# Loading K and V by whole batches in a one-core decode kernel: 2 MB transfers with 16 KB rows, and P written with zeros between its head groups

## The chip, the cores and the metric

The kernel runs on one core of a Trainium2 chip. Its time is the device time of one execution in microseconds (us); three executions of the kernel before gave 121.77, 121.84 and 121.88, a median of 121.84 us. Engine names: PE does matrix products (PEld is its weight load), DVE is the vector engine, ACT the scalar engine, POOL the third elementwise engine, SP the engine that issues most transfers.

## What is computed

One decode step for 8 batches: a layer norm, attention over the last 1024 positions of a cache (32 query heads on 8 key/value heads of 128 elements), a gated feed-forward network, and a product of the two. All inputs are bf16.

```python
W = min(4096, max(256, Sk // 4))                       # Sk = 4096, so W = 1024
q = (x @ wq).reshape(B, Sq, Hq, Dh)                    # x: 8 x 1 x 512, normalised; wq: 512 x 4096
k = jnp.repeat(k_cache[:, :, Sk - W:, :], rep, axis=1) # cache: 8 x 8 x 4096 x 128, rep = 4
v = jnp.repeat(v_cache[:, :, Sk - W:, :], rep, axis=1)
p = _softmax(jnp.einsum("bhqd,bhkd->bhqk", q, k) * (Dh ** -0.5))
s = jnp.einsum("bhqk,bhkd->bhqd", p, v).reshape(B, Sq, Hq * Dh) @ wo
g = _silu((_gelu(xn @ w_gate) * (xn @ w_up)) @ w_down) # F = 1792
out = x + s * g
```

Each batch brings 2 MB of K and 2 MB of V (MB here is 2^20 bytes where transfers are counted), wq and wo are 4 MB each, the three FFN weights 1.75 MB each: 47.5 million bytes in all, each read once.

## The kernel before, in words

**Storage.** A ring of 16 slots of 128 partitions by 8 KB (1 MB) takes everything that comes by a large transfer. The 8 key/value heads are split into two groups g of 4 (HG = 4, NG = 2). A transfer of `load_cache` (L71) brings one group of K or V of one batch: partition p holds 32 consecutive positions of one head, an 8 KB row. wq comes as four transfers of 1 MB (L94), one for each slice k of the contraction; gate, up and down in two transfers of 0.875 MB each (L425, L433), wo in three of 1 MB and three smaller pieces of the last (L443). SP issues them in the order K0, wq, K1, V0, K2, V1, K3, V2, ... K7, V6, V7, gate, up, down, wo. A transfer waits for the last reader of its slot, and also for the landing of the transfer eight before it, because eight completion semaphores go round.

**Order of the work.** The schedule is written out by hand (`manual_schedule`): each engine executes its instructions in the order of the program text, so an instruction that waits holds up everything behind it on its engine.

**Query.** 32 products of 128x512 (L247) build q in eight PSUM banks, slice k after slice k. Copies to bf16 (L256), DVE transposes (L259) and 16 small copies (L268, by DVE and ACT) make `qbd`, the stationary operand of the scores.

**A batch b** takes these steps:

- `turn_k(b, g)` (L235): a DVE transpose in 32x32 blocks turns a 1 MB group of K, read as 2048 words of 32 bits a partition, into `kT`. Three kT buffers.
- `scores(b, g)` (L283, L294): one masking product for each half of the 1024 columns of S with g = 0, then 8 products of 128x512 for each group. S is 128 partitions x 1024 columns in PSUM; a partition is one query head and one of 4 parts of the window.
- `softmax(b)`: the maximum of each row on DVE (L304), two small DVE steps across the four parts (L309, L311), four small ACT instructions that write the negative maximum `nb` (L314), then one ACT exponential of 128x1024 (L316) that writes P and its sums.
- `turn_p(b)` (L327): a DVE transpose of P, 512 words a partition.
- `values(b)` (L338): 64 products of 128x128. `keep_o` (L351) copies the result to SBUF, `gather` (L359, L363) sums the parts on PE, and after four batches `regroup` (L374 to L390) normalises on DVE, makes 8 small products and casts into `oT`.

The loop's order around the change:

```python
    for b in range(B):
        if b + 2 < B:
            load_k(b + 2)
        if b + 1 < B:
            load_v(b + 1)
            turn_k(b + 1, 0)
        softmax(b)
        if b + 1 < B:
            scores(b + 1, 0)
        if b >= 1:
            gather(b - 1)
        if b + 1 < B:
            turn_k(b + 1, 1)
            scores(b + 1, 1)
        turn_p(b); values(b); keep_o(b)
        if b == 4:
            regroup(0)
```

**Tail.** After the last batch PE does gather(7) and regroup(1), then the products z and u of the FFN (L457, 16 each), waits for the gelu chain on ACT and DVE (L467 to L480), does the 56 products of f (L486), and last the 128 products of s (L505), 32 for each megabyte of wo in the order of its pieces. Two DVE steps (L513, L515) and the output transfer (L517) end the kernel.

Of the kernel before, what the change touches and what calls it, by code (L numbers as in the profile page):

```python
# [7 lines left out]
ACT = mybir.ActivationFunctionType  # L8
# [7 lines left out]
N_SLOTS = 16  # L16
# [5 lines left out]
def kernel(  # L22
# [27 lines left out]
    C = W * HG // P  # L50
    ROW = C * Dh
    FT = F // 4
# [16 lines left out]
    def load_cache(cache, b, g, name):  # L69
        t = slot(name)  # L70
        nc.sync.dma_start(  # L71
            out=t,
            in_=cache[b, g * HG : (g + 1) * HG, win0:Sk, :].rearrange(
                "n (p c) d -> p n (c d)", c=C
            ),
        )
        return t
# [3 lines left out]
    def load_k(b):  # L81
        for g in range(NG):
            k_sb[b, g] = load_cache(A_k_cache, b, g, "k_sb")

    def load_v(b):
        for g in range(NG):
            v_sb[b, g] = load_cache(A_v_cache, b, g, "v_sb")
# [4 lines left out]
    for k in range(NK):  # L92
        t = slot("wq_sb")
        nc.sync.dma_start(out=t, in_=wq_v[:, k, :])  # L94
        wq_sb.append(t)
# [109 lines left out]
    sel = consts.tile([P, NG, Hq], FP32, name="sel")  # L205
    nc.vector.memset(sel, 0.0)
    for g in range(NG):
        nc.vector.tensor_reduce(
            out=sel[:, g, g * qd : (g + 1) * qd],
            in_=ident.rearrange("p (t g h) -> p g h t", t=4, g=NG)[:, g],  # L210
            axis=AX.X,
            op=ALU.add,
        )
# [19 lines left out]
    def turn_k(b, g):  # L233
        t = kT_pool.tile([P, ROW], BF16, name="kT")
        nc.vector.transpose(out=t.bitcast(I32), in_=k_sb[b, g].bitcast(I32))  # L235
        kT[b, g] = t
# [4 lines left out]
    q_bf = slot("q_bf")  # L241
    q_t = slot("q_t")
    with tc.tile_pool(name="ps_q", bufs=1, space=PSUM) as ps_q:
        q_ps = [ps_q.tile([P, 512], FP32, name=f"q_ps{i}") for i in range(8)]
        for k in range(NK):
            for i in range(8):
                nc.tensor.matmul(  # L247
                    q_ps[i],
                    xnR[:, k, :, :].rearrange("p j b -> p (j b)"),
                    wq_sb[k][:, i * 512 : (i + 1) * 512],  # L250
                    start=(k == 0),
                    stop=(k == NK - 1),
                )
        for i in range(8):
            e = nc.vector.tensor_copy if i % 2 else nc.scalar.copy
            e(out=q_bf[:, i * 512 : (i + 1) * 512], in_=q_ps[i])  # L256
            if i % 2:
                sl = slice((i - 1) * 512, (i + 1) * 512)
                nc.vector.transpose(out=q_t[:, sl].bitcast(I32), in_=q_bf[:, sl].bitcast(I32))  # L259

    q_v = q_t.rearrange("p (g h m b r w) -> p m b r w g h", g=NG, h=qd, m=2, b=B, r=RB)
    for j in range(4):
        sl = slice(32 * j, 32 * j + 32)
        for m in range(2):
            e = (nc.vector.tensor_copy, nc.scalar.copy)[(j + m) % 2]
            for g in range(NG):
                c0 = j * Hq + g * qd
                e(out=qbd[sl, m, :, :, g, c0 : c0 + qd], in_=q_v[sl, m, :, 0, :, g, :])  # L268
# [3 lines left out]
    sums = keep.tile([P, B], FP32, name="sums")  # L272
# [6 lines left out]
    def scores(b, g):  # L279
        if g == 0:  # L280
            S[b] = ps_s.tile([P, 2, 512], FP32, name="S_ps")
            for half in range(2):
                nc.tensor.matmul(  # L283
                    S[b][:, half, :],
                    neg_st.rearrange("p j h -> p (j h)"),
                    neg_mv.rearrange("p a n -> p (a n)"),
                    start=True,
                    stop=False,
                )
        kv = kT[b, g].rearrange("p (c m i w) -> p c m i w", m=2, i=32, w=2)  # L290
        for m in range(2):
            for w in range(2):
                for half in range(2):
                    nc.tensor.matmul(  # L294
                        S[b][:, half, :],
                        qbd[:, m, b, w, g, :],
                        kv[:, half * 16 : (half + 1) * 16, m, :, w],
                        start=False,
                        stop=(g == NG - 1 and m == 1 and w == 1),
                    )  # L300

    def softmax(b):
        mx = two.tile([P, 1], FP32, name="mx")
        nc.vector.tensor_reduce(  # L304
            out=mx, in_=S[b].rearrange("p a c -> p (a c)"), axis=AX.X, op=ALU.max
        )

        m2 = two.tile([64, 1], FP32, name="m2")
        nc.vector.tensor_tensor(out=m2, in0=mx[0:64, :], in1=mx[64:128, :], op=ALU.max)  # L309
        m1 = two.tile([32, 1], FP32, name="m1")  # L310
        nc.vector.tensor_tensor(out=m1, in0=m2[0:32, :], in1=m2[32:64, :], op=ALU.max)  # L311
        nb = two.tile([P, 1], FP32, name="nb")
        for j in range(4):
            nc.scalar.mul(nb[32 * j : 32 * j + 32, :], m1, -inv)  # L314
        P_sb[b] = two.tile([P, C // 2, 32, 2], BF16, name="P_sb")
        nc.scalar.activation(  # L316
            out=P_sb[b].rearrange("p c i w -> p c w i"),
            in_=S[b].rearrange("p a (c w i) -> p (a c) w i", w=2, i=32),
            func=ACT.Exp,
            bias=nb,  # L320
            scale=inv,
            accum_out=sums[:, b : b + 1],
        )

    def turn_p(b):
        pT[b] = two.tile([P, C // 2, Hq, 2], BF16, name="pT")
        nc.vector.transpose(  # L327
            out=pT[b].rearrange("p c h w -> p (c h w)").bitcast(I32),
            in_=P_sb[b].rearrange("p c i w -> p (c i w)").bitcast(I32),
        )  # L330

    def values(b):
        O_ps[b] = ps_o.tile([P, NG, Dh], FP32, name="O_ps")
        for g in range(NG):
            vv = v_sb[b, g].rearrange("p (c d) -> p c d", d=Dh)
            for c in range(C):
                t = c % 4
                nc.tensor.matmul(  # L338
                    O_ps[b][32 * t : 32 * t + 32, g, :],
                    pT[b][:, c // 2, :, c % 2],  # L340
                    vv[:, c, :],
                    start=(c < 4),
                    stop=(c >= C - 4),
                )
# [4 lines left out]
    def keep_o(b):  # L349
        O_sb[b] = two.tile([P, NG, Dh], FP32, name="O_sb")  # L350
        nc.scalar.copy(out=O_sb[b], in_=O_ps[b])  # L351

    def gather(b):
        q = b % 4
        if q == 0:
            o_ps[b // 4] = ps_g.tile([P, Dh + 1], FP32, name="o_ps")
        o = o_ps[b // 4][32 * q : 32 * q + 32, :]
        for g in range(NG):
            nc.tensor.matmul(  # L359
                o[:, 0:Dh], sel[:, g, :], O_sb[b][:, g, :], start=(g == 0), stop=(g == NG - 1)  # L360
            )
        for g in range(NG):
            nc.tensor.matmul(  # L363
                o[:, Dh : Dh + 1],
                sel[:, g, :],
                sums[:, b : b + 1],
                start=(g == 0),
                stop=(g == NG - 1),
            )

    def regroup(q):

        rc = two.tile([P, 1], FP32, name="rc")
        nc.vector.reciprocal(out=rc, in_=o_ps[q][:, Dh : Dh + 1])  # L374
# [21 lines left out]
    scores(0, 1)  # L396
    for b in range(B):
        if b + 2 < B:
            load_k(b + 2)
        if b + 1 < B:  # L400
            load_v(b + 1)
            turn_k(b + 1, 0)
        softmax(b)
        if b + 1 < B:
            scores(b + 1, 0)
        if b >= 1:
            gather(b - 1)
        if b + 1 < B:
            turn_k(b + 1, 1)
            scores(b + 1, 1)  # L410
# [7 lines left out]
    HR = NK // 2  # L418
    wgu = []
    for w in (B_w_gate, B_w_up):  # L420
        wv = w.rearrange("(p k) f -> p k f", k=NK)
        for i in range(2):
            t = slot("wgu_sb")
            tv = t[:, 0 : HR * F].rearrange("p (k f) -> p k f", k=HR)
            nc.sync.dma_start(out=tv, in_=wv[:, i * HR : (i + 1) * HR, :])  # L425
            wgu.append(tv)
    wd = []
    wdv = B_w_down.rearrange("(p j) d -> p j d", j=NJ)
    for i in range(2):
        t = slot("wd_sb")  # L430
        n = NJ // 2
        tv = t[:, 0 : n * D].rearrange("p (j d) -> p j d", d=D)
        nc.sync.dma_start(out=tv, in_=wdv[:, i * n : (i + 1) * n, :])  # L433
        wd.append(tv)
    wo = []
    for u in range(NU):
        t = slot("wo_sb").rearrange("p (j d) -> p j d", d=D)
# [15 lines left out]
    for n, ws in (("z_ps", wgu[0:2]), ("u_ps", wgu[2:4])):  # L453
        ps = ps_f.tile([P, FT], FP32, name=n)
        for k in range(NK):
            for t in range(4):
# [3 lines left out]
                    ws[k // HR][:, k % HR, t * FT : (t + 1) * FT],  # L460
# [23 lines left out]
    for j in range(NJ):  # L484
        for t in range(4):
# [3 lines left out]
                wd[j // (NJ // 2)][:, j % (NJ // 2), t * DT : (t + 1) * DT],  # L489
# [60 lines left out]
```

## Time and profile before

| what | value |
|---|---|
| device time, median of 3 executions | 121.84 us (121.77 to 121.88) |
| the profiled execution: span from its first to its last instruction | 119.9 us (119.85) |
| median less that span: what lies around the instructions | 1.99 us |
| PE busy, DVE busy, ACT busy | 72.9, 76.5, 32.3 us |
| transfers on SP's queue, share of 16 DMA engines' span | 94.5% |
| bytes moved | 47.46 million, 396 GB/s over the span |
| from issue to landing of a 1 MB K or V transfer, median | 19.6 us |
| slowest engine of 16: landing of K6 whole, of K7 whole, of V7 whole | 73.53, 83.35, 93.15 us |

No device time of the profiled execution itself is listed apart from its span, so the 1.99 us are counted as constant. The landings are the times of the completion semaphores' last updates in the trace, from the span's start. In the page's rows "busy, mean ns" are of a group of equal instructions; "idle before" is the idle time of the engine ahead of them and what ended it. In timeline rows the first column is the start and the second the length, in us; a bracket holds the idle time before.

### The profile page before, as it was taken

Reading aid. Unit: us, or ns where it says so; the run is one execution under the profiler, and the core shown is the slowest. Engines: PE = TensorE matmul, PEld = TensorE weight load, DVE = VectorE, ACT = ScalarE, POOL = GpSimd, SP = SyncE. Lnnn points to the kernel's source line nnn. Section 1 sums busy time; section 2 is a strip of 40 time slices with the busy share of each in tenths; the row PEclk is TensorE's granted clock in tenths of the full one; section 3 lists DMA queues with packets and bytes.
Section 4 is the critical chain, followed back from the end, with each engine's and each line's share of the span. In section 5 each row is a group of like instructions: output and inputs, shape, how many; then the busy total and the mean of one; then the engine's idle time right before and its main releaser. Section 6 shows DMA issues by size and latency. Waiting matters only on the chain.

```text
span 119.9 us, 2323 instructions
## 1 busy us (share of the span) xinstructions
PE 72.9 (61%) x992; PEld 38.0 (32%) x992; DVE 76.5 (64%) x100; ACT 32.3 (27%) x76; POOL 3.2 (3%) x10
## 2 busy tenths in 40 slices
PE   0103999033994997969687684992692547353460
PEld 0101333001341543535443351450352432052440
DVE  3698824999039999999959959909951253720010
ACT  4600005358007052341712510700608101100000
POOL 2250000000000000000000000000000000000000
PEclk9999999955589999999999999599999855555555
DMA  2999999999999999999999999999999999999920
GB/s 90 399 410 427 429 435 418 429 427 435 413 432 429 427 424 418 432 427 421 424 427 427 432 421 416 429 432 429 413 427 432 423 419 419 433 433 418 403 109 3
DMA packets 6974, 47.61 MB, mean 397 GB/s; under 512 B 812, under 2 KB 948, under 8 KB 1972
## 3 DMA queue, kind: packets, MB, share of 16 engines
q1 hardware_dynamic: 6948, 47.46, 94.5%
q8 instruction: 7, 0.11, 0.3%
q14 instruction: 3, 0.02, 0.0%
q10 hardware_dynamic: 16, 0.01, 0.0%
HBM read 47.46 MB, written 0.01 MB: 396 GB/s over the span
## 4 chain that ended last, share of the span: by engine, by line
DMA 52%; DVE 19%; PE 15%; ACT 8%; issue 1%; SPq 1%; DVEq 0%
DMA k_sb<-in_A_k_cache_dram 16%; DMA wgu_sb<-in_B_w_up_dram 16%; DMA wo_sb<-in_A_wo_dram 13%; DVE kT L235 7%; DMA wq_sb<-in_A_wq_dram 7%; PE q_ps L247 7%; PE S_ps L294 7%; DVE mx L304 4%; ACT P_sb L316 4%; ACT qbd L268 3%; DVE q_t L259 2%; DVE q_bf L256 2%; ACT nb L314 2%; DVE pT L327 2%; SPq L71 1%
## 5 line engine op out<-in xcount | busy, mean ns | idle before, releaser
L294 PE MATMUL S_ps<-kT,qbd 128*128 128x512 bf16 x128 | 33.5, 408 | 15.7 <-DVE kT L235 12.3
L235 DVE STREAM_TRANSPOSE kT<-k_sb 128x2048 int32<-128x2048 int32 x16 | 36.5, 2289 | 4.3 <-DMA k_sb<-in_A_k_cache_dram 4.2
L294 PEld LDWEIGHTS <-qbd 128*128 128x128 bf16 x128 | 12.9, 102 | 33.2 <-issue 17.0
L247 PE MATMUL q_ps<-wq_sb,xnR 128*128 128x512 bf16 x32 | 9.9, 483 | 6.2 <-DMA wq_sb<-in_A_wq_dram 6.2
L304 DVE TENSOR_REDUCE mx<-S_ps 128x1 f32<-128x1024 f32 x8 | 9.6, 1195 | 5.9 <-PE S_ps L294 5.9
L314 ACT ACTIVATE nb<-m 32x1 f32<-32x1 f32 x32 | 6.4, 201 | 21.9 <-DVE m L311 21.7
L316 ACT ACTIVATE P_sb<-S_ps,nb 128x1024 bf16<-128x1024 f32 x8 | 11.1, 1390 | 0.3
L338 PE MATMUL O_ps<-v_sb,pT 128*32 128x128 bf16 x512 | 8.6, 220 | 2.6 <-DVE pT L327 2.6
L351 ACT COPY O_sb<-O_ps 128x256 f32<-128x256 f32 x8 | 3.0, 372 | 22.6 <-PE O_ps L338 22.6
L338 PEld LDWEIGHTS <-pT 128*32 128x32 bf16 x512 | 7.2, 97 | 5.6 <-issue 3.0
L327 DVE STREAM_TRANSPOSE pT<-P_sb 128x512 int32<-128x512 int32 x8 | 5.7, 711 | 3.4 <-ACT P_sb L316 3.3
L283 PE MATMUL S_ps<-neg_mv,neg_st 128*128 128x512 bf16 x16 | 5.2, 410 | 3.8 <-DVE q_bf L256 3.8
L247 PEld LDWEIGHTS <-xnR 128*128 128x128 bf16 x32 | 3.7, 118 | 12.0 <-issue 10.2
L505 PE MATMUL s_ps<-wo_sb,oT 128*32 128x128 bf16 x128 | 4.4, 307 | 4.7 <-DMA wo_sb<-in_A_wo_dram 4.7
L359 PE MATMUL o_ps<-O_sb,sel 128*32 128x128 f32 x32 | 5.9, 314 | 1.0 <-ACT O_sb L351 1.0
L256 ACT CAST q_bf<-q_ps 128x512 bf16<-128x512 f32 x4 | 2.1, 600 | 14.2 <-PE q_ps L247 14.2
L268 ACT COPY qbd<-q_t 32x256 bf16<-32x256 bf16 x8 | 4.7, 622 | 3.3 <-DVE q_t L259 3.3
L513 DVE TENSOR_TENSOR y<-s_ps,g_sb 128x128 f32<-128x128 f32 x1 | 0.3, 292 | 8.1 <-PE s_ps L505 8.1
L505 PEld LDWEIGHTS <-oT 128*32 128x32 bf16 x128 | 3.5, 136 | 5.6 <-issue 5.6
L256 DVE CAST q_bf<-q_ps 128x512 bf16<-128x512 f32 x4 | 2.6, 662 | 3.9 <-PE q_ps L247 3.9
L359 PEld LDWEIGHTS o_ps<-O_sb,sel 128*32 128x32 f32 x32 | 3.2, 121 | 4.4 <-issue 2.1
L240 DVE MEMSET qbd<- 128x4096 uint32 x1 | 3.5, 3472 | 0.8 <-issue 0.8
(64 smaller groups left out, 47.1 us busy)
## 6 DMA issues: line engine op xcount, KB each, us to landing
k_sb<-in_A_k_cache_dram SPq DMA_DIRECT2D x16, 1024.0 KB, 19.6
v_sb<-in_A_v_cache_dram SPq DMA_DIRECT2D x16, 1024.0 KB, 19.6
wq_sb<-in_A_wq_dram SPq DMA_DIRECT2D x4, 1024.0 KB, 11.5
wo_sb<-in_A_wo_dram SPq DMA_DIRECT2D x3, 1024.0 KB, 17.8
wgu_sb<-in_B_w_gate_dram SPq DMA_DIRECT2D x2, 896.0 KB, 19.1
wgu_sb<-in_B_w_up_dram SPq DMA_DIRECT2D x2, 896.0 KB, 18.7
wd_sb<-in_B_w_down_dram SPq DMA_DIRECT2D x2, 896.0 KB, 17.8
wo_sb<-in_A_wo_dram SPq DMA_DIRECT2D x1, 512.0 KB, 16.7
```

The lines of the kernel that those rows point to most:

```text
L235: nc.vector.transpose(out=t.bitcast(I32), in_=k_sb[b, g].bitcast(I32))
L247: nc.tensor.matmul(q_ps[i], xnR[:, k, :, :].rearrange("p j b -> p (j b)"), wq_sb[k][:, i * 512 : (i + 1) * 512], start=(k == 0), stop=(k = ...
L256: e(out=q_bf[:, i * 512 : (i + 1) * 512], in_=q_ps[i])
L268: e(out=qbd[sl, m, :, :, g, c0 : c0 + qd], in_=q_v[sl, m, :, 0, :, g, :])
L294: nc.tensor.matmul(S[b][:, half, :], qbd[:, m, b, w, g, :], kv[:, half * 16 : (half + 1) * 16, m, :, w], start=False, stop=(g == NG - 1 an ...
L304: nc.vector.tensor_reduce(out=mx, in_=S[b].rearrange("p a c -> p (a c)"), axis=AX.X, op=ALU.max)
L314: nc.scalar.mul(nb[32 * j : 32 * j + 32, :], m1, -inv)
L316: nc.scalar.activation(out=P_sb[b].rearrange("p c i w -> p c w i"), in_=S[b].rearrange("p a (c w i) -> p (a c) w i", w=2, i=32), func=ACT.Exp,
L327: nc.vector.transpose(out=pT[b].rearrange("p c h w -> p (c h w)").bitcast(I32), in_=P_sb[b].rearrange("p c i w -> p (c i w)").bitcast(I32),)
L338: nc.tensor.matmul(O_ps[b][32 * t : 32 * t + 32, g, :], pT[b][:, c // 2, :, c % 2], vv[:, c, :], start=(c < 4), stop=(c >= C - 4),)
L359: nc.tensor.matmul(o[:, 0:Dh], sel[:, g, :], O_sb[b][:, g, :], start=(g == 0), stop=(g == NG - 1))
L505: nc.tensor.matmul(s_ps[32 * t : 32 * t + 32, :], oT[:, j, u, :], wo[u][:, j, t * DT : (t + 1) * DT], start=(u == 0 and j == 0), stop=(u = ...
```

## The change

K and V of a batch come in one transfer of 2 MB each: partition p holds 64 positions of one head (a 16 KB row), and the head index runs over 8 values within 128 partitions. The ring has 8 slots of 2 MB. `turn_k(b, half)` takes half of each row, so both halves need the whole transfer. A half now holds keys of both head groups; `scores(b, half)` fills one half of S's columns with 8 products, 4 for each group, whose moving operand runs over 4 neighbouring heads, then steps on. A row of S holds, as before, the scores of one query head with the 4 heads of its own group; in P's layout all 8 heads stand side by side. So the exponential is done twice, once for each group, over all 1024 columns: `nb` has two columns, and the column of the other group is so low that zeros are written (`off`, `mg`). P is twice as long (1024 words a partition in `turn_p`). `values` still makes 64 products, into one 128x128 result; `gather` needs half as many products; `regroup` adds the two sums first.

In the loop, `softmax` is split into `top` and `softmax`; `turn_k(1, 0)` stands ahead of the loop, and in batch b the DVE order is `top(b)`, `turn_k(b+1, 1)`, `turn_k(b+2, 0)`, `turn_p(b)`. wq comes in two transfers of 2 MB, gate, up and down in one of 1.75 MB each, wo in the same six pieces; q's two buffers share a slot, and q's copies and the qbd copies are dealt out differently between ACT and DVE (6 and 2, then 5 and 11).

The diff, cut to its core:

```diff
-N_SLOTS = 16
+N_SLOTS = 8
...
-    C = W * HG // P
+    C = W * Hkv // P
     ROW = C * Dh
+    HALF = ROW // 2
+    KB = 32 // Hkv
...
+            in_=cache[b, :, win0:Sk, :].rearrange("n (p c) d -> p n (c d)", c=C),
...
+    for i in range(2):
+        t = slot("wq_sb").rearrange("p (k n) -> p k n", k=NK // 2)
+        nc.sync.dma_start(out=t, in_=wq_v[:, i * (NK // 2) : (i + 1) * (NK // 2), :])
+        wq_sb += [t[:, k, :] for k in range(NK // 2)]
...
-    def turn_k(b, g):
-        t = kT_pool.tile([P, ROW], BF16, name="kT")
-        nc.vector.transpose(out=t.bitcast(I32), in_=k_sb[b, g].bitcast(I32))
+    def turn_k(b, half):
+        t = kT_pool.tile([P, HALF], BF16, name="kT")
+        nc.vector.transpose(
+            out=t.bitcast(I32), in_=k_sb[b][:, half * HALF : (half + 1) * HALF].bitcast(I32)
+        )
...
-                        kv[:, half * 16 : (half + 1) * 16, m, :, w],
+                        kv[:, :, m, :, g * HG : (g + 1) * HG, w],
...
+        mg = two.tile([Hq, NG], FP32, name="mg")
+        nc.vector.tensor_scalar(
+            out=mg, in0=off, scalar1=m1[:, 0:1], scalar2=-inv, op0=ALU.add, op1=ALU.mult
+        )
+        nb[b] = two.tile([P, NG], FP32, name="nb")
         for j in range(4):
-            nc.scalar.mul(nb[32 * j : 32 * j + 32, :], m1, -inv)
...
+            nc.scalar.copy(out=nb[b][32 * j : 32 * j + 32, :], in_=mg)
+
+    def softmax(b):
+        P_sb[b] = two.tile([P, C // 2, KB, Hkv, 2], BF16, name="P_sb")
+        for g in range(NG):
+            nc.scalar.activation(
+                out=P_sb[b].rearrange("p c k n w -> p w (c k) n")[:, :, :, g * HG : (g + 1) * HG],
+                in_=S[b].rearrange("p w (c n) -> p w c n", n=HG),
+                func=ACT.Exp,
+                bias=nb[b][:, g : g + 1],
+                scale=inv,
+                accum_out=sums[:, b, g : g + 1],
+            )
...
     def regroup(q):
 
         rc = two.tile([P, 1], FP32, name="rc")
-        nc.vector.reciprocal(out=rc, in_=o_ps[q][:, Dh : Dh + 1])
+        nc.vector.tensor_reduce(
+            out=rc, in_=o_ps[q][:, Dh : Dh + NG], axis=AX.X, op=ALU.add
+        )
+        nc.vector.reciprocal(out=rc, in_=rc)
...
     scores(0, 0)
     scores(0, 1)
+    turn_k(1, 0)
     for b in range(B):
         if b + 2 < B:
             load_k(b + 2)
         if b + 1 < B:
             load_v(b + 1)
-            turn_k(b + 1, 0)
+        top(b)
         softmax(b)
         if b + 1 < B:
             scores(b + 1, 0)
+            turn_k(b + 1, 1)
+            scores(b + 1, 1)
+        if b + 2 < B:
+            turn_k(b + 2, 0)
         if b >= 1:
             gather(b - 1)
-        if b + 1 < B:
-            turn_k(b + 1, 1)
-            scores(b + 1, 1)
         turn_p(b)
...
-        for i in range(2):
-            t = slot("wgu_sb")
-            tv = t[:, 0 : HR * F].rearrange("p (k f) -> p k f", k=HR)
-            nc.sync.dma_start(out=tv, in_=wv[:, i * HR : (i + 1) * HR, :])
-            wgu.append(tv)
...
+        tv = slot("wgu_sb")[:, 0 : NK * F].rearrange("p (k f) -> p k f", k=NK)
+        nc.sync.dma_start(out=tv, in_=w.rearrange("(p k) f -> p k f", k=NK))
+        wgu.append(tv)
+    wd = slot("wd_sb")[:, 0 : NJ * D].rearrange("p (j d) -> p j d", d=D)
+    nc.sync.dma_start(out=wd, in_=B_w_down.rearrange("(p j) d -> p j d", j=NJ))
```

More of the change, by code (lines that the diff above doesn't have):

```diff
@@ L67, with load_cache @@
     nc.scalar.dma_start(out=x_sb, in_=A_x.flatten_outer_dims())
-    def load_cache(cache, b, g, name):
+    def load_cache(cache, b, name):
         t = slot(name)
@@ L72, in load_cache @@
             out=t,
-            in_=cache[b, g * HG : (g + 1) * HG, win0:Sk, :].rearrange(
-                "n (p c) d -> p n (c d)", c=C
-            ),
+            in_=cache[b, :, win0:Sk, :].rearrange("n (p c) d -> p n (c d)", c=C),
         )
@@ L81, in load_k @@
     def load_k(b):
-        for g in range(NG):
-            k_sb[b, g] = load_cache(A_k_cache, b, g, "k_sb")
+        k_sb[b] = load_cache(A_k_cache, b, "k_sb")
     def load_v(b):
-        for g in range(NG):
-            v_sb[b, g] = load_cache(A_v_cache, b, g, "v_sb")
+        v_sb[b] = load_cache(A_v_cache, b, "v_sb")
     load_k(0)
@@ L91 @@
     wq_sb = []
[L92 to L95, printed above, removed]
+    for i in range(2):
+        t = slot("wq_sb").rearrange("p (k n) -> p k n", k=NK // 2)
+        nc.sync.dma_start(out=t, in_=wq_v[:, i * (NK // 2) : (i + 1) * (NK // 2), :])
+        wq_sb += [t[:, k, :] for k in range(NK // 2)]
     load_k(1)
@@ L204 @@
     NU = Hq // 8
-    sel = consts.tile([P, NG, Hq], FP32, name="sel")
-    nc.vector.memset(sel, 0.0)
-    for g in range(NG):
[L208 to L212, printed above, removed]
+    sel = consts.tile([P, Hq], FP32, name="sel")
+    nc.vector.tensor_reduce(
+        out=sel, in_=ident.rearrange("p (t h) -> p h t", t=4), axis=AX.X, op=ALU.add
+    )
+    off = consts.tile([Hq, NG], FP32, name="off")
+    nc.vector.memset(off, -NEG)
+    for g in range(NG):
+        nc.gpsimd.affine_select(
+            out=off[:, g : g + 1],
+            in_=off[:, g : g + 1],
+            compare_op=ALU.is_ge,
+            fill=0.0,
+            base=(-qd if g == 0 else qd - 1),
+            pattern=[[0, 1]],
+            channel_multiplier=(1 if g == 0 else -1),
         )
@@ L231 @@
     kT = {}
-    def turn_k(b, g):
-        t = kT_pool.tile([P, ROW], BF16, name="kT")
-        nc.vector.transpose(out=t.bitcast(I32), in_=k_sb[b, g].bitcast(I32))
-        kT[b, g] = t
+    def turn_k(b, half):
[3 more added lines that the diff above has]
+        )
+        kT[b, half] = t
     turn_k(0, 0)
@@ L240 @@
     nc.vector.memset(qbd, 0.0)
-    q_bf = slot("q_bf")
-    q_t = slot("q_t")
+    q_both = slot("q_both")
+    q_bf = q_both[:, 0:HALF]
+    q_t = q_both[:, HALF:ROW]
     with tc.tile_pool(name="ps_q", bufs=1, space=PSUM) as ps_q:
@@ L253 @@
                 )
[L254 to L258, printed above, removed]
+        for half in range(2):
+            for i in range(4 * half, 4 * half + 4):
+                e = nc.vector.tensor_copy if i % 4 == 3 else nc.scalar.copy
+                e(out=q_bf[:, i * 512 : (i + 1) * 512], in_=q_ps[i])
+            for i in range(4 * half, 4 * half + 4, 2):
+                sl = slice(i * 512, (i + 2) * 512)
                 nc.vector.transpose(out=q_t[:, sl].bitcast(I32), in_=q_bf[:, sl].bitcast(I32))
@@ L264 @@
         for m in range(2):
-            e = (nc.vector.tensor_copy, nc.scalar.copy)[(j + m) % 2]
             for g in range(NG):
+                e = nc.scalar.copy if (4 * j + 2 * m + g) % 3 == 2 else nc.vector.tensor_copy
                 c0 = j * Hq + g * qd
@@ L271 @@
     pT, S, P_sb, O_ps = {}, {}, {}, {}
-    sums = keep.tile([P, B], FP32, name="sums")
+    sums = keep.tile([P, B, NG], FP32, name="sums")
     actx = ExitStack()
@@ L277, with scores @@
     ps_g = actx.enter_context(tc.tile_pool(name="ps_g", bufs=1, space=PSUM))
-    def scores(b, g):
-        if g == 0:
+    def scores(b, half):
+        if half == 0:
             S[b] = ps_s.tile([P, 2, 512], FP32, name="S_ps")
[L282 to L293, printed above, removed]
+        nc.tensor.matmul(
+            S[b][:, half, :],
+            neg_st.rearrange("p j h -> p (j h)"),
+            neg_mv.rearrange("p a n -> p (a n)"),
+            start=True,
+            stop=False,
+        )
+        kv = kT[b, half].rearrange("p (c m k n w) -> p c m k n w", m=2, k=KB, n=Hkv, w=2)
+        for g in range(NG):
+            for m in range(2):
+                for w in range(2):
                     nc.tensor.matmul(
@@ L300, in scores, with top @@
                     )
-    def softmax(b):
+    nb = {}
+    def top(b):
         mx = two.tile([P, 1], FP32, name="mx")
@@ L309, in softmax @@
         nc.vector.tensor_tensor(out=m2, in0=mx[0:64, :], in1=mx[64:128, :], op=ALU.max)
-        m1 = two.tile([32, 1], FP32, name="m1")
+        m1 = two.tile([Hq, 1], FP32, name="m1")
         nc.vector.tensor_tensor(out=m1, in0=m2[0:32, :], in1=m2[32:64, :], op=ALU.max)
-        nb = two.tile([P, 1], FP32, name="nb")
-        for j in range(4):
-            nc.scalar.mul(nb[32 * j : 32 * j + 32, :], m1, -inv)
[L315 to L323, printed above, removed]
+        mg = two.tile([Hq, NG], FP32, name="mg")
[3 more added lines that the diff above has]
+        nb[b] = two.tile([P, NG], FP32, name="nb")
+        for j in range(4):
+            nc.scalar.copy(out=nb[b][32 * j : 32 * j + 32, :], in_=mg)
+    def softmax(b):
+        P_sb[b] = two.tile([P, C // 2, KB, Hkv, 2], BF16, name="P_sb")
+        for g in range(NG):
+            nc.scalar.activation(
[5 more added lines that the diff above has]
+                accum_out=sums[:, b, g : g + 1],
+            )
     def turn_p(b):
@@ L328, in turn_p @@
             out=pT[b].rearrange("p c h w -> p (c h w)").bitcast(I32),
-            in_=P_sb[b].rearrange("p c i w -> p (c i w)").bitcast(I32),
+            in_=P_sb[b].rearrange("p c k n w -> p (c k n w)").bitcast(I32),
         )
     def values(b):
[L333 to L344, printed above, removed]
+        O_ps[b] = ps_o.tile([P, Dh], FP32, name="O_ps")
+        vv = v_sb[b].rearrange("p (c d) -> p c d", d=Dh)
+        for c in range(C):
+            t = c % 4
+            nc.tensor.matmul(
+                O_ps[b][32 * t : 32 * t + 32, :],
+                pT[b][:, c % (C // 2), :, c // (C // 2)],
+                vv[:, c, :],
+                start=(c < 4),
+                stop=(c >= C - 4),
+            )
     o_ps = {}
@@ L349, in keep_o @@
     def keep_o(b):
-        O_sb[b] = two.tile([P, NG, Dh], FP32, name="O_sb")
+        O_sb[b] = two.tile([P, Dh], FP32, name="O_sb")
         nc.scalar.copy(out=O_sb[b], in_=O_ps[b])
@@ L355, in gather @@
         if q == 0:
-            o_ps[b // 4] = ps_g.tile([P, Dh + 1], FP32, name="o_ps")
+            o_ps[b // 4] = ps_g.tile([P, Dh + NG], FP32, name="o_ps")
         o = o_ps[b // 4][32 * q : 32 * q + 32, :]
[L358 to L369, printed above, removed]
+        nc.tensor.matmul(o[:, 0:Dh], sel, O_sb[b], start=True, stop=True)
+        nc.tensor.matmul(o[:, Dh : Dh + NG], sel, sums[:, b, :], start=True, stop=True)
     def regroup(q):
         rc = two.tile([P, 1], FP32, name="rc")
-        nc.vector.reciprocal(out=rc, in_=o_ps[q][:, Dh : Dh + 1])
+        nc.vector.tensor_reduce(
+            out=rc, in_=o_ps[q][:, Dh : Dh + NG], axis=AX.X, op=ALU.add
+        )
+        nc.vector.reciprocal(out=rc, in_=rc)
         o_x = two.tile([P, 8, Dh], BF16, name="o_x")
@@ L415 @@
             regroup(0)
-    HR = NK // 2
     wgu = []
     for w in (B_w_gate, B_w_up):
-        wv = w.rearrange("(p k) f -> p k f", k=NK)
-        for i in range(2):
-            t = slot("wgu_sb")
-            tv = t[:, 0 : HR * F].rearrange("p (k f) -> p k f", k=HR)
-            nc.sync.dma_start(out=tv, in_=wv[:, i * HR : (i + 1) * HR, :])
-            wgu.append(tv)
[L427 to L434, printed above, removed]
+        tv = slot("wgu_sb")[:, 0 : NK * F].rearrange("p (k f) -> p k f", k=NK)
[3 more added lines that the diff above has]
+    nc.sync.dma_start(out=wd, in_=B_w_down.rearrange("(p j) d -> p j d", j=NJ))
     wo = []
     for u in range(NU):
-        t = slot("wo_sb").rearrange("p (j d) -> p j d", d=D)
+        if u % 2 == 0:
+            pair = slot("wo_sb").rearrange("p (v j d) -> p v j d", v=2, d=D)
+        t = pair[:, u % 2]
         src = A_wo[u * 1024 : (u + 1) * 1024, :].rearrange("(p j) d -> p j d", j=8)
@@ L452 @@
     zu = []
-    for n, ws in (("z_ps", wgu[0:2]), ("u_ps", wgu[2:4])):
+    for n, ws in (("z_ps", wgu[0]), ("u_ps", wgu[1])):
         ps = ps_f.tile([P, FT], FP32, name=n)
@@ L459 @@
                     xnR[:, k, t, :],
-                    ws[k // HR][:, k % HR, t * FT : (t + 1) * FT],
+                    ws[:, k, t * FT : (t + 1) * FT],
                     start=(k == 0),
@@ L488 @@
                 hT[:, j, :],
-                wd[j // (NJ // 2)][:, j % (NJ // 2), t * DT : (t + 1) * DT],
+                wd[:, j, t * DT : (t + 1) * DT],
                 start=(j == 0),
```

## The prediction, made before the changed kernel was run

> **What bounds the kernel now.** I read the slices of the page first, then the chain in order of time, then DVE's and PE's timeline from 60 us on.
>
> ```profile
> PEclk9999999955589999999999999599999855555555
> DMA  2999999999999999999999999999999999999920
> GB/s 90 399 410 427 429 435 418 429 427 435 413 432 429 427 424 418 432 427 421 424 427 427 432 421 416 429 432 429 413 427 432 423 419 419 433 433 418 403 109 3
> ```
>
> The 16 DMA engines are full from 2 us to 115 us at about 427 GB/s. The time is the start, 47.46 million bytes at that rate, and an end.
>
> ```profile
> 61.38 19.52 DMA k_sb<-in_A_k_cache_dram
> ...
> 80.96 18.73 DMA wgu_sb<-in_B_w_up_dram
> ...
> 99.70 15.93 DMA wo_sb<-in_A_wo_dram
> 115.63 0.04 issue
> 115.67 0.66 PE s_ps L505 x16
> ```
>
> From 61 us the chain is transfers alone, up to the last piece of wo, whose products close it. But compute isn't far behind:
>
> ```profile
> 80.92 2.31 DVE L235 STREAM_TRANSPOSE kT<-k_sb 128x2048 int32<-128x2048 int32 x1 [2.85 <-DMA k_sb<-in_A_k_cache_dram]
> 88.92 1.23 DVE L304 TENSOR_REDUCE mx<-S_ps 128x1 f32<-128x1024 f32 x1 [1.12 <-PE S_ps L294]
> 98.60 1.68 PE L457 MATMUL z_ps<-wgu_sb,xnR 128*32 128x448 bf16 x16
> 105.58 1.68 PE L486 MATMUL f_ps<-wd_sb,hT 128*32 128x128 bf16 x56 [2.68 <-DVE hT L480]
> 108.58 1.04 PE L505 MATMUL s_ps<-wo_sb,oT 128*32 128x128 bf16 x32 [1.31 <-DMA wo_sb<-in_A_wo_dram]
> ```
>
> K7's first megabyte starts the last stretch of attention at 80.92; its FFN begins at 98.60 and ends at 107.26; PE waits only 1.31 us for wo. Without any wait the four parts of s (4 x 1.04 = 4.16) would end at 107.26 + 0.05 + 4.16 = 111.5, against 116.33 in fact. So **the cover of the compute tail is 4.8 us**, and whatever delays z by more sets the end.
>
> **The change, part by part.**
>
> *Transfers.* The trace's packet records show 46, 159 and 309 ns for 1, 4 and 8 KB: 37.6 ns a KB and some 8.4 ns fixed. Landings in the steady stretch are 2.445 us apart for a megabyte (K4 to K6: 19.52 us for 8), where 64 KB an engine at 37.6 ns make 2.405; 0.040 us are fixed. Rows of 16 KB and half the transfers halve that: 36 MB of K, V and wq save 36 x 0.020 = 0.72, the FFN weights 3 x 0.037 = 0.11, together **0.83 us**. Bounds: 0 if a 16 KB row goes as two packets; 1.60 if the packet records' fixed part is saved whole (144 + 24 packets fewer an engine at 8.4 ns, 21 completion packets at 9 ns). I take 0.83, from the landings, which are what others wait for. [...]
>
> *SP's queue.* The count in flight falls from 8 of 1 MB to at most 7 or 8 of 2 MB, and each now waits for its slot's reader alone. The tightest of these: wo's first piece waits for `turn_k(6,1)`, about 84 us below, and its turn on the engines comes about 102. So the rings never run dry; if that cover failed, each missing microsecond would show whole.
>
> *Landing of K.* Before, `turn_k(b,0)` began with the first megabyte (K7: 80.89); now with the second (83.35, less 0.64 = 82.7). That is 1.8 us later for K7, about the same for K6 (71.09; 73.53 - 0.56 = 73.0).
>
> *Start.* wq's first landing moves from 10.86 to 13.37. 16 products at 427 ns would end about 19, wq's rest lands about 18, 16 more at 213 ns end near 21.5 (20.85 before). Copies: six of 0.60 on ACT beside two casts and four transposes on DVE (2 x 0.66 + 4 x 0.71), then qbd 11 x 0.33 on DVE beside 5 x 0.57 on ACT: ends near 29, as before. One masking product moves between the halves, 0.4. All this disappears: DVE waits for K5 and K6 below by 0.7 and 2.3 us.
>
> *A batch on DVE.* `mx` 1.20, m2 and m1 0.155 and 0.147, `mg` new: two columns, 0.16 by those rows; with gaps **top = 1.79**. Two kT of 2.24 (back to back; 2.3 after a wait). pT: from 711 ns for 512 words and 2289 for 2048, 1.03 ns a word, **1.24** for 1024 (bounds 0.71 and 1.42). A batch takes 7.5 instead of the 6.76 between the maxima at 41.87, 48.63 and 55.39.
>
> *ACT.* nb 0.84 stays (4 x 0.20), the exponential of 1.45 runs twice: 0.86 + 2.90 = **3.76**. Bounds of one: 1.39 is the same operation on as many elements; a copy with scattered reads and writes (qbd, 622 ns for 256 columns) takes 1.67 times the contiguous one (O_sb, 372 ns), so up to 2.3; 0.7 if zeros cost nothing. I take 1.45: its output steps by 4 bytes in both kernels. Mid-loop it lies beside two kT (4.48); in batches 6 and 7, with one and none, it is bare.
>
> *PE.* As many S and value products; runs of 4 heads in the moving operand have no row; bounds 1 and 1.37 times (weight load of scattered o_x 162 ns, of xnR 118), hidden in the slack of a batch, since 16 x 0.213 + 0.6 + 1.1 + 0.4 = 5.5 of 7.5. `gather` halves: -0.4, as O_sb's copy -0.1.
>
> *The new wait.* `turn_k(b+2,0)` waits for K(b+2), and `turn_p(b)`, hence values(b), regroup(0) and top(b+1), stand behind it on DVE. DVE comes to `turn_k(6,0)` at 63.2 (K5) + 2.24 + 1.24 + 1.79 + 2.24 = 70.7 and waits until 73.0. From there:
>
> - kT(6,0) 75.3; pT(4) 76.5; regroup(0): two small steps 0.33, o_x 1.28, products 0.71, cast 0.48, and part of values(4) ahead of them at the lower clock: 79.7
> - top(5) 81.5; kT(6,1) 83.7; kT(7,0) 86.0 (K7 landed at 82.7); pT(5) 87.2; top(6) 89.0
> - nb and two exponentials 92.75 (kT(7,1) beside them); pT(6) 94.0; top(7) 95.8; nb and exponentials 99.55; pT(7) 100.8
> - values(7) 1.08 at full clock, double at half; 1.6 taken: 102.4; O_sb, gather, sums, o_x, r_ps: 0.28 + 0.75 + 0.33 + 1.34 + 0.6: z at **105.7**, 7.1 later than 98.60.
>
> From K7's landing alone the same durations give 82.7 + 22.1 = 104.8. Then z to f's end as before, 8.66: 114.4; s 4.2: 118.5, with all of wo landed (115.96 - 0.83). The output's 3.52 us after s stay: span 122.1, against 119.85: **+2.25**. With the 1.99 around it as in the median shown, 121.84 + 2.25 = **124.1 us**.
>
> PE's clock is a second cost. The page shows 5 for PEclk in the slice at 75 us, after 2.2 us of idle PE (71.35 to 73.56), and from 96 us on. Now each K wait leaves it idle about as long or longer. [...] In my sum only values(4), values(7) and gather carry it; s may regain full clock at its end, up to -1.
>
> **Rivals.**
>
> - *Transfers stay last*: 121.84 - 0.83 = 121.0 (120.2 with 1.60). For it: full slices, 4.8 us of cover. It decides when z slips by less than 4.8 - 0.8 = 4.0, z before 102.6. Against it: K7's landing, two bare exponentials and a longer pT allow 104.8; it needs engines' skew at K7 gone (its first engine finished 1.5 us before the last) and cheaper exponentials.
> - *PE or ACT becomes the bound* (slower side): exponentials at 2.3 instead of 1.45 add 1.7 to each of batches 6 and 7, 3.4: 127.5; half clock in scores adds 1.9 for a half batch on the path: 126.
> - *Rows are cut to 8 KB, no gain in transfers*: K6 and K7 land 0.6 later, 124.7; slower just the same.
>
> **How the numbers follow.** Forecast, compute tail last, 122.3 to 125.5: 0.62. PE or ACT bound, 125.5 to 130: 0.20. Transfers last or compute just beside them, 120.2 to 121.6: 0.13. Between, about equal: 0.05. A measurement of this kernel can tell 0.2%, 0.24 us. Faster 0.13, same 0.05, slower 0.82. The range leaves out about half of the first rival and a good third of the second: 121.3 to 127.0.
>
> **What would show it.** Right: PE waits for wo in no part of s; DMA slices fall to 0 while PE still works; DVE waits for K5 and K6 with pT queued behind; two exponentials of 1.4 and pT of 1.24; z at 104 to 107. Packets of 16 KB at 610 ns and K6 landing at 73.0 confirm the first term. Wrong: s still waiting for wo's last piece, or z before 102.6; an exponential or S product far from its row of before.

## The result, and the profile after

The changed kernel took 196.36 us (median of four executions, 195.49 to 198.38) against 121.86 us: a ratio of 1.613, interval 1.603 to 1.623. The forecast was 124.1, with a range up to 127.0. The profiled execution has a span of 194.1 us and took 195.86.

The slices of the page of the changed kernel, each now 4.85 us long:

```profile
PEclk9999997599559755885579559755885699555555
DMA  6999999999999999999999999999999999999980
GB/s 164 216 321 432 327 216 216 216 226 221 223 223 233 216 223 216 216 218 216 216 216 219 216 216 216 216 223 216 216 219 219 216 233 213 359 426 420 430 354 7
```

The DMA engines are as busy as before, at half the rate: 216 to 233 GB/s in nearly every slice. Two stretches stand out: around the fourth slice, where wq comes, and from the 35th on, where the FFN weights and wo come. There it is up to 432. DVE waits for each K from K2 on, for 8.1 to 12.4 us; three of these waits:

```profile
51.36 2.31 DVE L240 STREAM_TRANSPOSE kT<-k_sb 128x2048 int32<-128x2048 int32 x1 [8.14 <-DMA k_sb<-in_A_k_cache_dram]
90.45 2.31 DVE L240 STREAM_TRANSPOSE kT<-k_sb 128x2048 int32<-128x2048 int32 x1 [11.90 <-DMA k_sb<-in_A_k_cache_dram]
109.76 2.31 DVE L240 STREAM_TRANSPOSE kT<-k_sb 128x2048 int32<-128x2048 int32 x1 [11.93 <-DMA k_sb<-in_A_k_cache_dram]
```

The idle time in the bracket, some 12 us for each of K3 to K6, stands where the kernel before waited 1.38 us for K5 and 2.85 for K7 (the row at 80.92 in the prediction):

```profile
61.34 2.31 DVE L235 STREAM_TRANSPOSE kT<-k_sb 128x2048 int32<-128x2048 int32 x1 [1.38 <-DMA k_sb<-in_A_k_cache_dram]
```

The tail of the changed kernel on PE, with the first products of s at its end:

```profile
180.56 1.68 PE L489 MATMUL f_ps<-wd_sb,hT 128*32 128x128 bf16 x56 [2.56 <-DMA wd_sb<-in_B_w_down_dram]
182.98 1.04 PE L508 MATMUL s_ps<-wo_sb,oT 128*32 128x128 bf16 x32 [0.74 <-DMA wo_sb<-in_A_wo_dram]
```

PE waits for the down weights and for wo, so the transfers are last, as before.

**Where the 74.5 us came from.** In the packet records the 16 KB rows of K and V take 1240 ns (median of the steady stretch) where those of wq take 611, and 14 KB rows of the FFN weights 535. K4 landed at 90.43 and K6 at 128.96: 38.53 us for 8 MB, 4.82 a megabyte against 2.445 before. For the 32 MB of K and V that is 32 x 2.37 = 75.9 us more, a little over the whole loss. V7 lands at 167.31 instead of 93.15; from there to the end it is 26.8 us, against 26.7 before.

### The profile page after: what moved, and what is told of

Read it like the earlier page. It is cut to its first block, busy times and chain, and to the rows that moved or that the text cites. A ratio compares the mean times of both kernels' runs of the same rounds, so it can differ in the third digit from the quotient of the medians.

```text
span 194.1 us, 2240 instructions
## 1 busy us (share of the span) xinstructions
PE 78.9 (41%) x953; PEld 41.7 (22%) x960; DVE 81.5 (42%) x110; ACT 39.7 (20%) x91; POOL 3.4 (2%) x12
## 3 DMA queue, kind: packets, MB, share of 16 engines
q1 hardware_dynamic: 3924, 47.46, 96.6%
## 4 chain that ended last, share of the span: by engine, by line
DMA 36%; another core or an unknown queue 36%; DVE 21%; PE 3%; SPq 2%; issue 1%
DMA k_sb<-in_A_k_cache_dram 24%; DVE kT L240 13%; DMA wo_sb<-in_A_wo_dram 12%; DVE pT L344 3%; DVE mx L314 3%; PE O_ps L354 2%; SPq L73 1%; DVE mg L323 1%; SPq L92 1%; DVE m L319 0%; DVE m L321 0%; SPq L446 0%; PE s_ps L508 0%; PE r_ps L396 0%
## 5 line engine op out<-in xcount | busy, mean ns | idle before, releaser
L354 PE MATMUL O_ps<-v_sb,pT 128*32 128x128 bf16 x512 | 14.4, 300 | 74.5 <-DVE pT L344 55.3
L302 PE MATMUL S_ps<-kT,qbd 128*128 128x512 bf16 x128 | 38.6, 453 | 7.4 <-DVE qbd L277 3.6
L354 PEld LDWEIGHTS <-pT 128*32 128x32 bf16 x512 | 12.3, 138 | 75.5 <-DVE pT L344 56.2
L333 ACT ACTIVATE P_sb<-S_ps,nb 128x1024 bf16<-128x1024 f32 x16 | 21.1, 1349 | 0.3
L344 DVE STREAM_TRANSPOSE pT<-P_sb 128x1024 int32<-128x1024 int32 x8 | 9.7, 1214 | 5.3 <-ACT P_sb L333 5.3
L328 ACT COPY nb<-mg 32x2 f32<-32x2 f32 x32 | 6.1, 190 | 12.3 <-DVE mg L323 12.0
L265 ACT CAST q_both<-q_ps 128x512 bf16<-128x512 f32 x6 | 3.0, 611 | 19.8 <-PE q_ps L255 19.8
L374 PE MATMUL o_ps<-O_sb,sel 128*32 128x128 f32 x16 | 3.5, 302 | 0.7 <-ACT O_sb L367 0.7
L277 DVE COPY qbd<-q_both 32x256 bf16<-32x256 bf16 x11 | 3.4, 359 | 0.0
L277 ACT COPY qbd<-q_both 32x256 bf16<-32x256 bf16 x5 | 3.0, 617 | 0.9 <-DVE q_both L268 0.9
```

Of the source, the lines that this page charges most:

```text
L302: nc.tensor.matmul(S[b][:, half, :], qbd[:, m, b, w, g, :], kv[:, :, m, :, g * HG : (g + 1) * HG, w], start=False, stop=(g == NG - 1 and m ...
L328: nc.scalar.copy(out=nb[b][32 * j : 32 * j + 32, :], in_=mg)
L333: nc.scalar.activation(out=P_sb[b].rearrange("p c k n w -> p w (c k) n")[:, :, :, g * HG : (g + 1) * HG], in_=S[b].rearrange("p w (c n) -> ...
L344: nc.vector.transpose(out=pT[b].rearrange("p c h w -> p (c h w)").bitcast(I32), in_=P_sb[b].rearrange("p c k n w -> p (c k n w)").bitcast( ...
L354: nc.tensor.matmul(O_ps[b][32 * t : 32 * t + 32, :], pT[b][:, c % (C // 2), :, c // (C // 2)], vv[:, c, :], start=(c < 4), stop=(c >= C - 4),)
```

## The experiments

The row of 16 KB can't be slow by itself, since wq has it too, at 611 ns. What K and V alone have is the way their rows are laid over the partitions. Three theories: **A**, the grouping of the destination: 16 groups of 8 partitions instead of 32 groups of 4. **B**, long rows of the cache. **C**, the source addresses (16 KB and 1 MB apart) collide.

### Groups of 4 with 16 KB rows

The changed kernel reads 4 heads of 2048 positions instead of 8 heads of 1024; nothing else differs.

```diff
-            in_=cache[b, :, win0:Sk, :].rearrange("n (p c) d -> p n (c d)", c=C),
+            in_=cache[b, 0:4, Sk - 2 * W : Sk, :].rearrange("n (p c) d -> p n (c d)", c=C),
```

> The changed kernel, but each K or V transfer reads 4 heads x 2048 positions instead of 8 heads x 1024: still 2 MB in 16 KB rows, but the destination's 128 partitions are 32 groups of 4 instead of 16 groups of 8. (It reads other cache rows than the reference; the instructions are otherwise the same.) Theory A (the grouping of partitions 16 x 8 halves the rate, because two DMA engines at a time write where only one can): K packets fall from 1240 to about 611 ns, 2 MB land every 4.85 us, and the time is set by the compute tail as predicted, 124.1 us (122.3 to 125.5). Theory B (16 KB rows of the cache are slow themselves, by their length): stays near 196 us, packets 1240 ns. Theory C (the source addresses, 16 KB and 1 MB apart, collide in HBM): the steps are the same here with 4 heads, so it stays well above 150 us. If attention's compute isn't bound after all: 121.0 us.

121.63 us (ten executions, 121.29 to 122.47), a ratio to the kernel before of 0.9993, interval 0.9974 to 1.0011. The loss is gone. The time is below the 122.3 to 125.5 that the compute tail was to bring; the part on the prediction comes back to it. The slices of its page:

```profile
DMA  2999999999999999999999999999999999999600
GB/s 90 434 413 434 424 429 434 435 435 435 429 429 435 432 429 413 429 429 426 435 424 429 435 418 435 429 435 424 429 429 439 409 447 428 404 426 418 271 0 3
```

Packets of 16 KB take 611 ns, at the 5th and at the 95th of a hundred alike, and the rate is that of before or a little above. B falls, and C is unlikely. The end of the GB/s row, "271 0 3", is new: wo has landed at 114.96, 5.7 us before the end of the span, against 3.9 in the kernel before. Its profiled execution was the slowest of the ten, 122.47 us with a span of 120.7. PE's tail there:

```profile
105.11 1.68 PE L460 MATMUL z_ps<-wgu_sb,xnR 128*32 128x448 bf16 x16
...
112.09 1.68 PE L489 MATMUL f_ps<-wd_sb,hT 128*32 128x128 bf16 x56 [3.80 <-DVE hT L483]
113.56 3.59 PE L508 MATMUL s_ps<-wo_sb,oT 128*32 128x128 bf16 x128
```

The 128 products of s run in one stretch, with no wait for wo between them: in this execution the compute tail is last. z starts at 105.11, for which the forecast had 105.7. It is the changed kernel's computation with the transfers at the speed that the prediction gave them.

### The same destination, a near source

```diff
+            in_=cache[b]
+            .rearrange("n s d -> (n s) d")[0 : 16 * 9 * C, :]
+            .rearrange("(p r c) d -> p r (c d)", r=9, c=C)[:, 0:8, :],
```

> The changed kernel with its own destination (16 groups of 8 partitions, 16 KB rows), but a source that lies close together: row r of group p at (9p + r) x 16 KB in one batch's cache, no step of 1 MB. (It reads other cache rows than the reference.) Theory A (destination): unchanged, packets about 1240 ns, 190 to 200 us. Theory C (source addresses collide): packets fall to about 611 ns and the time to 121 to 126 us. Theory B (row length): 190 to 200 us.

197.44 and 200.55 us in two executions, packets at 1238 ns by the median. The source is now 2.25 MB in one piece, and nothing got better. C falls.

### The kernel before, with 16 groups of 8

Its 1 MB transfers and 8 KB rows stay; one brings 8 heads of 512 positions.

```diff
-            in_=cache[b, g * HG : (g + 1) * HG, win0:Sk, :].rearrange(
+            in_=cache[b, :, win0 + g * W // 2 : win0 + (g + 1) * W // 2, :].rearrange(
```

> The kernel before with its 1 MB transfers and 8 KB rows, but each brings 8 heads x 512 positions, so that its partitions are 16 groups of 8 instead of 32 groups of 4. (The heads then stand at other partitions than the masks assume; instructions are the same.) Theory A: K packets double from 309 to about 620 ns, 1 MB lands every 4.8 us, and the time rises to 190 to 200 us, with nothing else of the change made. Theory B (row length of 16 KB): 121.9 us as before. Theory C: between, by how the nearer source addresses (8 KB and 1 MB apart) collide.

192.93 us, ratio 1.583 (1.579 to 1.587). Its slices:

```profile
DMA  5999999999999999999999999999999999999980
GB/s 139 219 302 432 355 218 221 219 219 219 219 221 219 221 221 219 219 219 219 221 226 230 226 230 230 226 225 237 223 240 225 228 238 228 369 428 423 430 350 10
```

The reader sees the changed kernel's picture with none of its other edits: K and V at 218 to 240 GB/s, packets of 8 KB at 605 ns by the median of all (620 from 40 to 150 us), with wq at 432 in between. The grouping alone carries 71.2 of the 74.5 us. A stands, with one reservation: the order in which the source's rows are read (16 x 8 or 32 x 4) goes with the partitions' grouping in every run, so no run parts these two; the near source changed the rows' addresses only.

### Fewer groups in a transfer: halves and quarters

To see what in the grouping costs, each 2 MB went, with the same data and layout, as n transfers of 128/n partitions (n = 2, then 4).

```diff
+        for h in range(2):
+            nc.sync.dma_start(
+                out=t[h * P // 2 : (h + 1) * P // 2, :],
+                in_=cache[b, :, win0 + h * W // 2 : win0 + (h + 1) * W // 2, :].rearrange(
```

> The changed kernel, same layout and same data, but each 2 MB goes as two transfers of 64 partitions (8 groups of 8 partitions). [...] If the packets' doubling came of something that needs all 16 engines (a rate limit of the memory or of the path), 8 engines at 611 ns a packet: 2 MB in 9.8 us, about 196 us as now.

> The changed kernel, same layout and same data, but each 2 MB goes as four transfers of 32 partitions (4 groups of 8). [...] If groups of 8 partitions slow an engine by itself (each engine moving through 8 neighbouring partitions): packets stay at 1240 ns and the time is near 660 us.

Halves: 311.74 us. Quarters: 382.36 us, one execution each. The slices, halves first, quarters second:

```profile
DMA  5996554544555455454545545445889988775541
GB/s 137 201 146 195 186 119 110 119 119 119 119 119 121 119 119 119 119 133 121 146 140 150 152 157 167 144 161 165 182 175 224 182 226 178 194 173 213 220 209 57
```

```profile
DMA  5962222222222222222222222222222599867321
GB/s 135 217 165 108 105 110 108 105 110 108 105 109 110 105 108 109 107 108 108 105 110 108 105 112 108 105 110 108 107 110 107 158 216 217 205 172 191 149 106 47
```

Quarters: the engines are busy for a quarter (2 tenths; 4.0 packets under way at a time from 60 to 120 us), so it is as if 4 of 16 carried a transfer, and in the steady stretch packets take 611 ns, both at the 5th and the 95th of a hundred. Groups of 8 neighbouring partitions don't slow an engine by themselves. Halves: half the engines (8.1 packets at a time), and packets of 1256 ns (median, 60 to 120 us), not 611: 8 engines are enough for the slowdown, and it isn't a limit of the total rate, which is 119 GB/s there. Added up, such packets make about 350 us for both, an estimate: 16 of 1256 ns on each of 8 engines, or 32 of 611 on each of 4, are some 20 us for 2 MB and some 320 for K and V, and the other 13 MB at 2.445 a megabyte are some 30. Neither time is that. The halves were faster: from about 147 us on the rate lies between 140 and 226 GB/s, and from 120 to 240 us 242 of 1024 packets of 16 KB took under 620 ns, where from 60 to 120 none did; why is left open. The quarters were slower, at their end: the FFN weights' packets, which came beside the last of V, took 1022 ns by the median instead of 535.

Why packets in groups of 8 took 1240 ns with 16 engines and 1256 with 8, but 611 with 4, is not shown. That two engines write where only one can, as theory A has it, is a guess: the records here name neither engine nor partition, and no run kept the 16 groups of 8 and moved the engines to other places in them.

### The tail: without the second exponential

From the kernel with groups of 4, the second head group's exponential was left out (its P is not computed; two P buffers are set to zero once, ahead of the loop; those lines are not shown).

```diff
-        for g in range(NG):
+        for g in range(1):
```

> The kernel of the 32 groups of 4 (16 KB rows at full rate, other cache rows than the reference), with the second exponential of each batch left out (the second head group's P is not computed). Theory: its tail is compute-bound, z at 105.11 and s without a wait for wo. Without the second exponential each of batches 6 and 7 loses 1.4 us from the bare ACT stretch: z near 102, transfers last again, and the time falls by the excess over the transfers, to 120.9 us (121.84 less 0.83, up to 1.0 for the landing of wo at 114.96 instead of 115.96). If transfers or something else were the limit there, it stays at 121.6.

> The 32 groups of 4 with 16 KB rows again, on the same chip as the kernel without the second exponential, for comparison with it: 121.6 us (121.3 to 122.5 as the PE clock's steps fall).

Without it 120.56 us (120.50 to 120.73, six executions), ratio to the kernel before 0.988 (0.985 to 0.991); with it, on the same chip, 122.13 (120.87 to 122.47, twelve), ratio 0.9996 (0.9967 to 1.0025). The two series do not overlap. PE's tail without it:

```profile
103.40 1.68 PE L466 MATMUL z_ps<-wgu_sb,xnR 128*32 128x448 bf16 x16
...
111.80 2.73 PE L514 MATMUL s_ps<-wo_sb,oT 128*32 128x128 bf16 x112
114.90 0.61 PE L514 MATMUL s_ps<-wo_sb,oT 128*32 128x128 bf16 x16 [0.37 <-DMA wo_sb<-in_A_wo_dram]
```

z comes 1.7 us earlier (1.4 for each of the last two batches had been expected), and the last 16 products wait for wo again. So with full-rate transfers the tail did set the end in most executions, and leaving out the second exponential was enough to make the transfers last again.

### The weights' transfers alone

The kernel before with the new ring, wq in two transfers and the FFN weights in one each; K and V in 1 MB transfers in the two halves of a slot, with groups of 4.

```diff
+    for i in range(2):
+        t = slot("wq_sb").rearrange("p (k n) -> p k n", k=NK // 2)
+        nc.sync.dma_start(out=t, in_=wq_v[:, i * (NK // 2) : (i + 1) * (NK // 2), :])
...
+        tv = slot("wgu_sb")[:, 0 : NK * F].rearrange("p (k f) -> p k f", k=NK)
+        nc.sync.dma_start(out=tv, in_=w.rearrange("(p k) f -> p k f", k=NK))
```

> The kernel before with the change's ring (8 slots of 16 KB a partition), wq in two transfers of 2 MB, gate, up and down in one each, wo in its six pieces, and K and V as before (1 MB, 32 groups of 4, each pair in the halves of one slot). From the fixed 0.040 us a megabyte: wq saves 0.08 and the FFN weights 0.11, so 121.65 us, a ratio of 0.9985. If the later landing of wq's first part reached the end, it would be above 122.1; if packets' fixed 8.4 ns count whole, 121.4.

121.82 us beside 121.75, ratio 0.9999 (0.9983 to 1.0016). The interval holds both the 0.15% that was expected and nothing; the run decides nothing but that q's later start costs no time that shows.

## Why the prediction was wrong

- **The step that failed** is *Transfers*: "Rows of 16 KB and half the transfers halve that". It priced K's rows from packets and landings of the kernel before, whose K comes in groups of 4, and put the bounds at 0 and 1.60 us of gain, with no loss. The change has two edits there, the length of the rows and the partitions over which they go. The second got no term at all, though the diff shows it: C counts all 8 heads, so 16 groups of 8. In place of a gain of 0.83 stands a loss of 75.9 for K and V. The working for the length itself was right: 611 ns for 16 KB (610 stated), and with groups of 4 K6 landed at 72.88 (72.97 predicted) and wo at 114.96 (115.13).
- **The size of a transfer**, 2 MB instead of 1 MB, was weighed there, and its small gain was right: with groups of 4, wo landed at 114.96, 1.0 us earlier than the 115.96 before. But it was the wrong question: the profile before has no transfer of K or V in groups of 8 from which the loss could be priced.
- **What bounds the kernel now** was right, and the cover of the tail too: with full-rate transfers a z that came 6.5 us later ate the 4.8 us of cover, and the profiled span was 0.8 longer than before.
- **The compute tail** was right in its order and, K5's wait apart, near in its sizes, read in the profiled execution of the run with groups of 4: K waits of 2.43 and 2.32 us at K5 and K6 (0.7 and 2.3 predicted), pT 1.21 (1.24), `mg` 0.22 (0.16), two exponentials 2.70 (2.90), z 105.11 (105.7), f's end 113.77 (114.4). What was mis-sized is s: 3.59 instead of 4 x 1.04 = 4.16. The clock has little to do with it ("up to -1" was left out of the sum): it was granted at half until 116.98, and the last product ended at 117.15. At that clock 32 products took 1.04 and 128 in one stretch 3.59, which makes 0.85 for 32 and 0.19 once a stretch; the sum counted the 0.19 four times. Together that makes 120.7 of the 122.1 forecast for the span, in the slowest of ten executions; the median shows no difference from before at all. So even with its transfers as assumed, 124.1 was 2.0 to 2.5 us too much by the medians of the two series.

```profile
63.21 2.31 DVE L240 STREAM_TRANSPOSE kT<-k_sb 128x2048 int32<-128x2048 int32 x1 [2.43 <-DMA k_sb<-in_A_k_cache_dram]
66.70 1.90 PE L354 MATMUL O_ps<-v_sb,pT 128*32 128x128 bf16 x64 [3.60 <-DVE pT L344]
72.91 2.31 DVE L240 STREAM_TRANSPOSE kT<-k_sb 128x2048 int32<-128x2048 int32 x1 [2.32 <-DMA k_sb<-in_A_k_cache_dram]
76.40 1.08 PE L354 MATMUL O_ps<-v_sb,pT 128*32 128x128 bf16 x64 [1.44 <-DVE rc L380]
82.99 3.49 PE L302 MATMUL S_ps<-kT,qbd 128*128 128x512 bf16 x8 [2.39 <-DVE kT L240]
86.52 1.22 DVE L314 TENSOR_REDUCE mx<-S_ps 128x1 f32<-128x1024 f32 x1 [0.26 <-PE S_ps L302]
```

- **PE**: runs of 4 heads in the moving operand cost nothing (8 products of S in 1.89 to 1.90 us at full clock, as before). The clock fell around K waits, but not after every one: values at 66.70 took 1.90 us after 3.60 us of idle PE, those after K6's wait, at 76.40, 1.08; scores at 82.99 took 3.49 after 2.39 us of idle. The cost was nearly hidden: these scores held DVE's maximum up by 0.26 us. Before the change 8 such products took 2.49 us after 2.20 of idle PE (73.56) and 1.89 after 2.17 (83.28).
- **SP's queue** was right: the engines' slices stay full, with a median of 56 us (K) and 62 us (V) from issue to landing in the changed kernel. **The rivals** named rows cut to 8 KB, and waits in compute; none named a slower transfer.

## What to carry to other kernels

A transfer's price has to come from a row with the same grouping of partitions, not only the same size and row length. Groups of 4 partitions (32 of them) ran at about 430 GB/s in both row lengths, groups of 8 (16 of them) at about 220, with the engines shown as busy in both (94.5% of the span in the kernel before, 96.6% in the changed one). So a busy share near 1 does not tell the rate; compare nanoseconds a packet with another transfer of the same kernel.

## What the runs showed of the hardware that I had not expected

- The same 16 KB packet took 611 or 1240 ns, and an 8 KB packet 309 or 605, as its transfer went to 32 groups of 4 or to 16 of 8.
- Transfers of 4 groups kept as many as 4 of 16 engines busy at a time, those of 8 groups 8; 2 MB so cut took the kernel to 382 and 312 us.
- Where the compute tail sets the end or comes near it, the spans of twelve executions lay between 119.1 and 120.8 us; where transfers do, those of six without the second exponential between 118.7 and 119.0, and those of seventeen of the kernel before between 119.9 and 120.1. The whole times of the kernel before still spread from 121.64 to 122.75.
